# The second layer of chunk 1 in plain fp32 products, the second layer's weights split one block a place, and a reordered start in a DeltaNet + MoE kernel

## The chip, the cores and the metric

The kernel runs on one core of a Trainium2 chip. Its metric is the time of one execution on the device in microseconds (us), the median of several. The engines are TensorE (PE in the rows), VectorE (DVE), ScalarE (ACT), GpSimd (POOL) and SyncE (SP, which issues the transfers). Each engine works through its own list of instructions in order, and waits on semaphores for the others.

## What is computed

An attention with a delta rule, and on its output a two-layer perceptron with softplus (B = 4, H = 8, S = 768, head size 48, width 384, hidden width 2048):

```
k_n = k / (norm(k) + 1e-6)
for t in range(S):
    y[t]  = state . q[t]
    v_old = state . k_n[t]
    state = state + beta[t] * outer(k_n[t], v[t] - v_old)
x = y as (3072 tokens, 384)
g = softplus(x @ w_in)        # max(h, 0) + log1p(exp(-|h|)), w_in 384 x 2048
out = g @ w_out               # w_out 2048 x 384
```

## The kernel before, in words

**Attention in chunks.** The 768 steps are cut into 12 chunks of 64, and the 32 heads of a chunk are worked on together. A chunk needs its products of keys with keys (`gram`), the inverse of a triangular 64 x 64 system for each head, the corrected values, y and the next state. Two chunks share one inversion (`invert`). Its core is a chain of some 50 small pairs of instructions, `tmp` and `Z` (a multiply and an add), which for chunks 2 and up runs on POOL; for the first pair it runs on DVE. In front of the chain stand two wide multiplies by columns and by rows (L325, L327), which for `invert(1)` run on POOL and else on DVE, as does `scale_v(1)` (L146), which scales the values by the norms. Behind the chain come two transposes on DVE (L346, L349), and then products on PE in stages `cross_a`, `cross_b` whose results ACT copies into `off` and `tt`.

**The perceptron in places.** It is laid out in 96 "places" `t`, and all the attention's steps are hung on them with `at(place, cost, steps)`. The passes `PASSES` are chunk 0, chunk 1, and then two chunks at a time. Passes 0 and 1 have 8 places each, of two 128-row tiles of weights; the others have 16 places of one tile. A place on PE is `hidden` (first layer, L691), then the attention steps planned there, then `output` of the place before (second layer, L737), then steps planned at t + 0.5. On ACT a place is Abs, Exp and Ln of `hidden` (L696 to L698), then copies for the attention's steps, then the casts `high`. On DVE it is the rest of the softplus (L703 to L709), then `low`, then the attention's own.

**Split products.** Pass 0 multiplies plain fp32 numbers (two records of PE for each product in the trace). All passes after it multiply in a faster format, fp32r, with each number split in two: `hi` is a cast, `lo` what is left over, and three products take the place of one. For this a softplus of a split pass ends with a cast to `gh` (L705) and a subtract to `gl` (L706). The weights are split once, in `high` (a cast on ACT, 768 columns, w_in and w_out of a tile together) and `low` (a subtract on DVE, 768 columns), up to three tiles a place, in the places of the tables `HIGHS` and `LOWS` (places 3 to 13). The plain weights of tile f lie in a buffer named a{f+1}; `high(f)` writes buffer b{f} and `low(f)` buffer a{f}.

**The start.** Before place 0 stand the `gram` of chunks 2 and 3, the first mask's products (`first_p`), the inversion of the first pair on DVE, its solution by a sweep of small products, and `warm`, idle products that keep PE occupied. The weights come in through SP's queue in rows and are put together by DVE (`convert`, L648) during places 0 to 7.

Of the kernel before, what the change touches and what calls it, by code (L numbers as in the profile page):

```python
# [21 lines left out]
P = 128  # L22
# [21 lines left out]
CLEAR, DONE, END, GRAM, INV = {}, {1: 8, 2: 19}, {1: 6, 2: 17}, {4: 4, 5: 7}, {2: 11}  # L44
# [10 lines left out]
SLOT = (0, 2, 1)  # L55
FOUR = 15
# [4 lines left out]
def deltanet_moe(ctx, tc, kT, qT, kI, vN, beta, wts, out, outT):  # L61
# [83 lines left out]
    def scale_v(s):  # L145
        (nc.vector if s > 1 else nc.gpsimd).tensor_tensor(NV[s], NV[s], NN[s].unsqueeze(2).to_broadcast([P, NP, D]),  # L146
                                op=ALU.mult)
# [17 lines left out]
    def systems(u):  # L165

        LTD[u] = one.tile([P, 2 * NP, HB], F32, name="work")
# [128 lines left out]
    def invert(u):  # L296
# [27 lines left out]
        first = engine if u == N16 else nc.vector  # L324
        first.tensor_tensor(sq, sq, by_col, op=ALU.mult)  # L325
        yield 200 + n * n * m
        first.tensor_tensor(diagonal(Z, blocks, n, 0, 0, n, n), sq, by_row, op=ALU.mult)  # L327
# [46 lines left out]
    def couple(s):  # L374

        pms = [bank([P, NP // 2, C]) for e in range(2)]
        for i, e, p, ab, t in quads:
            nc.tensor.matmul(pms[e][tk[ab], i, :], LF[tk[t], s, p, :], DT[s][tk[t], p, :],
                             start=True, stop=True)
        negative(nc.scalar, MT[s][0], pms[0])  # L380
        negative(nc.scalar, MT[s][1], pms[1])
        for h in range(2):
            negative(nc.scalar, MT[s][2][tk[h]], pms[1][tk[1 - h]])
# [277 lines left out]
    def high(f):  # L661
        assert f < done[0]
        W[f, 0] = one.tile([P, 2 * DM], F32R, name=f"b{f}")
        nc.scalar.copy(W[f, 0], HF[f])

    def low(f):
        W[f, 1] = one.tile([P, 2 * DM], F32R, name=f"a{f}")
        nc.vector.tensor_tensor(W[f, 1], HF[f], W[f, 0], op=ALU.subtract)  # L668
# [5 lines left out]
    def weight(i, f, a, c, n):  # L674
        return W[f, a][:, c:c + n] if i else HF[f][:, c:c + n]
# [24 lines left out]
    def softplus(i, g):  # L700
        ph, a = PH.pop((i, g)), A.pop((i, g))
        if i:
            nc.vector.scalar_tensor_tensor(a, ph, 0.0, a, op0=ALU.max, op1=ALU.add)  # L703
            hi_lo = G[i, g] = [two.tile([P, 2 * n], F32R, name=name) for name in ("gh", "gl")]
            nc.vector.tensor_copy(hi_lo[0], a)  # L705
            nc.vector.tensor_tensor(hi_lo[1], a, hi_lo[0], op=ALU.subtract)  # L706
        else:
            hi_lo = G[i, g] = [two.tile([P, 2 * n], F32, name="gh")]
            nc.vector.scalar_tensor_tensor(hi_lo[0], ph, 0.0, a, op0=ALU.max, op1=ALU.add)  # L709
# [105 lines left out]
    with tc.manual_schedule(engines={ET.PE, ET.DVE, ET.Activation, ET.Pool, ET.SP}):  # L815
# [62 lines left out]
        both[0] = True  # L878
        pts = [first_p(0)]
        systems(1)  # L880
        gram(2)
        lower(1, halves_1[1], 1)
        gram(3)
        unread.append(ps_o.tile([P, 512], F32, name="po2"))
        warm(512)
        pts.append(first_p(1))
        run(iv)
        warm(512, 512)
# [4 lines left out]
        transpose_norms(0)  # L893
        for b, engine in enumerate((nc.scalar, nc.vector) * 2):
            expand(0, b, engine)
# [7 lines left out]
        couple(0)  # L903

        def pairs(g):
            return ([bank([P, 4, D]) for e in range(2)] if g == 0 else
                    [ps_h.tile([P, 4, D], F32, name=f"ph{e}") for e in range(2)])

        for g in range(2):
            i, to = slice(4 * g, 4 * g + 4), pairs(g)  # L910
            base(0, to, 4 * g, 4)
            nc.vector.tensor_copy(x_swap[:, i], to[1])
            nc.vector.tensor_copy(x_base[:, 0, i], to[0])
            for h in range(2):
                nc.gpsimd.tensor_copy(x_base[tk[h], 1, i], x_swap[tk[1 - h], i])
        warm(128)
# [17 lines left out]
        warm(256)  # L934
        first_y(0)
        warm(256)
        first_y(1)
        load_q(1)
        both[0] = False
# [94 lines left out]
        at(0, 6000, first_state, bind(steps, iv, 2))  # L1034
        at(0.5, 0, bind(steps, iv, 2))
        at(1, 1200, bind(couple, 1), bind(scale_v, 1), bind(run, iv))
# [15 lines left out]
        for c in range(2, NS, 2):  # L1052
# [30 lines left out]
            if u > 2:  # L1083
                if u == 3:
                    at(GRAM[c], 0, bind(load_beta, u), bind(systems, u), bind(gram_pair, c))
                at(8 * (c - 2) - (12 if u == 3 else EARLY), 0, bind(start, u, invert, INV[u]))
            elif u > 1:
                at(GRAM[c], 0, bind(load_beta, u), bind(systems, u), bind(gram, c))
                at(GRAM[c + 1], 0, bind(gram, c + 1), bind(start, u, invert, INV[u]))

        late, over = None, 0
        for t in range(8 * NS):
            costs[t] = costs.get(t, 0) + 960 * len(LOWS.get(t, ()))
            costs[t] += 1700 if t > 7 else 2900 if t < 5 else 700
        for i, p in enumerate(PASSES):
            for g in range(NF // 2 * len(p)):
# [15 lines left out]
                if i == 0:  # L1112
                    if g == 1:
                        load_v(2)
                        load_k(4)
                    top(2)
                for f in LOWS.get(t, ()):
                    low(f)
# [4 lines left out]
                for f in HIGHS.get(t, ()):  # L1123
                    high(f)
# [62 lines left out]
```

## Time and profile before

| what | value |
| --- | --- |
| runs | 562.95, 563.45, 563.60 us; median 563.45 |
| profiled execution | 562.74 us, of which 561.0 us are the span of the profile |
| PE busy | 539.0 us, 96% of the span |
| DVE, ACT, POOL busy | 65%, 65%, 37% |
| TensorE clock granted, mean | 0.988 |
| first hidden product (place 0) starts at | 40.45 us |

The span goes from the first to the last instruction on the core. An engine that isn't PE is idle for a third of the time or more, so only what PE waits for, or works at, can change the time; a time of a group of instructions elsewhere counts where it ends a wait of PE.

### The profile page before, as it was taken

To read this page: it belongs to the slowest core of one execution; us is meant where nothing else is said; L and a number is where in the kernel's file an instruction comes from. 1 tells how busy PE (TensorE), PEld (TensorE's weight loads), DVE (VectorE), ACT (ScalarE), POOL (GpSimd) and SP (SyncE) were. 2 spreads that over 40 slices of the span, in tenths; PEclk is the share of its full clock that TensorE was granted. 3 is DMA by queue.
4 is the path that set the end of the run, shared out by engine and by line. 5 is a ranking of instruction groups with operands and counts; after the bars stand their busy time and mean duration, and the time that the engine had idled before them with its cause. 6 is when DMAs were issued, how large, how long until landed. Compare 5 with 4: busy or idle time off the path is not lost.

```text
span 561.0 us, 17602 instructions
## 1 busy us (share of the span) xinstructions
PE 539.0 (96%) x7479; PEld 443.0 (79%) x7479; DVE 367.2 (65%) x660; ACT 363.9 (65%) x719; POOL 209.6 (37%) x365
## 2 busy tenths in 40 slices
PE   5788999899999999999999999999999999999997
PEld 3476768699987888877888888888887888888885
DVE  7858966999757857368747378747375737444434
ACT  5668685898677874756773757754557754454453
POOL 7125898119980179701886001886000000000000
PEclk9699999999999999999999999999999999999999
DMA  9919911223240132220122220031310030010001
GB/s 201 330 49 373 315 38 32 72 58 86 58 90 2 32 72 57 72 85 4 30 70 60 70 89 3 3 81 29 77 71 4 1 71 2 15 57 0 2 0 57
DMA packets 35502, 39.56 MB, mean 71 GB/s; under 512 B 22528, under 2 KB 25216, under 8 KB 35424
## 3 DMA queue, kind: packets, MB, share of 16 engines
q1 hardware_dynamic: 35280, 38.18, 24.2%
q8 instruction: 59, 0.97, 0.7%
q10 hardware_dynamic: 144, 0.26, 0.1%
q14 instruction: 19, 0.16, 0.1%
HBM read 31.55 MB, written 4.72 MB: 65 GB/s over the span
## 4 chain that ended last, share of the span: by engine, by line
PE 69%; POOL 16%; DVE 7%; DMA 3%; issue 2%; ACT 2%; ACTq 0%; DVEq 0%; POOLq 0%
PE po L737 29%; PE ph L691 27%; POOL Z L343 7%; POOL tmp L339 7%; PE pa L596 3%; PE pa L479 2%; DMA kt<-kT 2%; PE pa L439 2%; PE pa L565 1%; DMA big<-qT 1%; PE po L813 1%; DVE tt L349 1%; PE ph L577 1%; PE pa L577 1%; DVE a L668 1%
## 5 line engine op out<-in xcount | busy, mean ns | idle before, releaser
L691 PE MATMUL ph<-x,b 128*128 128x512 f32 (+1 forms) x576 | 166.2, 373 | 0.0
L696 ACT ACTIVATE a<-ph 128x512 f32<-128x512 f32 x96 | 57.4, 598 | 157.8 <-PE ph L691 153.2
L691 PE MATMUL ph<-x,a 128*128 128x512 f32 (+1 forms) x384 | 129.6, 374 | 2.4 <-DVE a L648 1.8
L703 DVE SCALAR_TENSOR_TENSOR a<-ph,a 128x512 f32<-128x512 f32 x88 | 60.4, 687 | 93.5 <-ACT a L698 93.2
L691 PEld LDWEIGHTS ph<-x,b 128*128 128x128 f32 x576 | 105.0, 188 | 19.4
L737 PE MATMUL po<-gh,b 128*128 128x512 f32 (+1 forms) x241 | 97.6, 405 | 1.4 <-DVE gh L705 1.4
L737 PE MATMUL po<-gh,a 128*128 128x512 f32 (+1 forms) x241 | 94.1, 390 | 0.0
L343 POOL TENSOR_TENSOR Z<-Z,tmp 128x30 f32<-128x30 f32 (+9 forms) x150 | 89.6, 597 | 11.8
L339 POOL TENSOR_TENSOR tmp<-Z,ltq 128x30 f32<-128x30 f32 (+9 forms) x150 | 86.5, 576 | 11.4
L691 PEld LDWEIGHTS ph<-x,a 128*128 128x128 f32 x384 | 72.0, 189 | 15.6 <-DVE a L648 2.2
L706 DVE TENSOR_TENSOR gl<-a,gh 128x512 fp32r<-128x512 f32 x88 | 66.4, 754 | 7.9 <-DVE gh L705 0.5
L737 PE MATMUL po<-gl,b 128*128 128x512 f32 (+1 forms) x241 | 69.4, 389 | 0.0
L698 ACT ACTIVATE a<-a 128x512 f32<-128x512 f32 x96 | 60.7, 632 | 3.1
L697 ACT ACTIVATE a<-a 128x512 f32<-128x512 f32 x96 | 60.6, 632 | 3.1
L737 PEld LDWEIGHTS po<-gh,b 128*128 128x128 f32 x241 | 45.2, 187 | 12.7 <-DVE gh L705 1.9
L737 PEld LDWEIGHTS po<-gl,b 128*128 128x128 f32 x241 | 45.2, 188 | 9.6
L737 PEld LDWEIGHTS po<-gh,a 128*128 128x128 f32 x241 | 45.3, 188 | 8.5
L705 DVE CAST gh<-a 128x512 fp32r<-128x512 f32 x88 | 40.0, 454 | 8.1 <-DVE a L703 0.9
L602 DVE TENSOR_TENSOR x<-pa,x 128x384 fp32r<-128x384 f32 x21 | 11.6, 554 | 38.1 <-ACT x L601 38.1
L256 POOL COPY ss<-ltq 128x32 f32<-128x32 f32 x6 | 1.4, 241 | 86.8 <-DVE ltq L303 86.8
L737 PE MATMUL po<-a,gh 128*128 128x384 f32 x96 | 33.5, 444 | 0.3 <-DVE gh L709 0.3
L493 DVE TENSOR_TENSOR big<-pa,maskP 64x256 f32<-64x256 f32 x66 | 27.8, 421 | 1.0
(220 smaller groups left out, 752.8 us busy)
## 6 DMA issues: line engine op xcount, KB each, us to landing
a<-wts SPq DMA_DIRECT2D x16, 383.8 KB, 7.5
b<-wts SPq DMA_DIRECT2D x16, 383.8 KB, 7.4
kt<-kT SPq DMA_DIRECT2D x24, 192.0 KB, 3.4
big<-qT SPq DMA_DIRECT2D x24, 192.0 KB, 4.0
nv<-vN SPq DMA_DIRECT2D x12, 384.0 KB, 3.7
ki<-kI SPq DMA_DIRECT2D x24, 192.0 KB, 3.3
outT<-ot SPq DMA_DIRECT2D x13, 256.0 KB, 2.3
x<-x SPq DMA_DIRECT2D x66, 32.0 KB, 2.0
```

Of the source, the lines that this page charges most:

```text
L339: engine.tensor_tensor(o, diagonal(Z, blocks, n, j + 1, j, r, j, (True, False)), diagonal(lq, blocks, n, j, 0, r, j, (False, True)), op=AL ...
L343: engine.tensor_tensor(z, z, o, op=ALU.add)
L493: nc.vector.tensor_tensor(be[tk[ab], ab, e, 4 * g:4 * g + 4, 0:C], pks[e][t, :, 0:C], maskP[t].unsqueeze(1).to_broadcast([C, 4, C]), op=AL ...
L596: nc.tensor.matmul(py[tk[ab], i, :], big[:, at + C:at + 2 * C], big[:, at:at + C], start=True, stop=True)
L691: nc.tensor.matmul(ph[:, j], weight(i, f, a, k * P, P), xr[b][k], start=(c == 0), stop=(c == len(terms) * NK - 1))
L696: nc.scalar.activation(a, ph, AF.Abs)
L697: nc.scalar.activation(a, a, AF.Exp, scale=-1.0)
L698: nc.scalar.activation(a, a, AF.Ln, bias=1.0)
L703: nc.vector.scalar_tensor_tensor(a, ph, 0.0, a, op0=ALU.max, op1=ALU.add)
L705: nc.vector.tensor_copy(hi_lo[0], a)
L706: nc.vector.tensor_tensor(hi_lo[1], a, hi_lo[0], op=ALU.subtract)
L737: nc.tensor.matmul(PO[i][h][:, c], l, r, start=(fs[j] == 0 and m == 0), stop=(fs[j] == NF - 1 and m == k - 1 and c != (cut and parts[0])))
```

## The change

The second layer of pass 1 (chunk 1) takes the plain form that pass 0 has: its softplus writes one fp32 `gh` without cast and subtract, and its output multiplies plain weights, one product in place of three. The split of a tile's weights is made in two halves, each in a buffer of its own with `hi` beside `lo`: w_in in buffer b{f} at the places of the old tables, and w_out in buffer a{f}, one tile a place, with the cast at place f + 12 and the subtract at place f + 13. The two wide multiplies of `invert(1)` and `scale_v(1)` go from POOL to DVE. K of chunk 4 and V of chunk 2 are loaded before 20 halves of weights are issued, and `gram(4)` moves from place 4 to 3.5. `invert(2)` starts at place 8.5 (it was 7). At the start, half of the first chain is set up ahead of `gram(2)`, one idle product of 512 columns changes its place, other idle products are trimmed or added (192 columns), a negative goes to DVE, one copy to ACT, and the sums of the base lie in other banks. The numbers of the planner's costs change with the smaller `low`.

```
@@ tables
-CLEAR, DONE, END, GRAM, INV = {}, {1: 8, 2: 19}, {1: 6, 2: 17}, {4: 4, 5: 7}, {2: 11}
+CLEAR, DONE, END, GRAM, INV = {}, {1: 8, 2: 19}, {1: 6, 2: 17}, {4: 3.5, 5: 7}, {2: 11}
+LATER = 13
@@ scale_v
-        (nc.vector if s > 1 else nc.gpsimd).tensor_tensor(NV[s], NV[s], NN[s].unsqueeze(2).to_broadcast([P, NP, D]),
+        nc.vector.tensor_tensor(NV[s], NV[s], NN[s].unsqueeze(2).to_broadcast([P, NP, D]),
@@ invert
-        first = engine if u == N16 else nc.vector
-        first.tensor_tensor(sq, sq, by_col, op=ALU.mult)
+        nc.vector.tensor_tensor(sq, sq, by_col, op=ALU.mult)
...
@@ couple
-        negative(nc.scalar, MT[s][1], pms[1])
-        for h in range(2):
-            negative(nc.scalar, MT[s][2][tk[h]], pms[1][tk[1 - h]])
+        negative(nc.scalar if s else nc.vector, MT[s][1], pms[1])
+        def rest():
+            for h in range(2):
+                negative(nc.scalar, MT[s][2][tk[h]], pms[1][tk[1 - h]])
+        return rest
@@ the split of the weights
-    def high(f):
+    def high(f, i):
         assert f < done[0]
-        W[f, 0] = one.tile([P, 2 * DM], F32R, name=f"b{f}")
-        nc.scalar.copy(W[f, 0], HF[f])
-    def low(f):
-        W[f, 1] = one.tile([P, 2 * DM], F32R, name=f"a{f}")
-        nc.vector.tensor_tensor(W[f, 1], HF[f], W[f, 0], op=ALU.subtract)
+        W[f, i] = one.tile([P, 2 * DM], F32R, name=f"{'ba'[i]}{f}")
+        nc.scalar.copy(W[f, i][:, 0:DM], HF[f][:, i * DM:(i + 1) * DM])
+    def low(f, i):
+        w = W[f, i]
+        nc.vector.tensor_tensor(w[:, DM:], HF[f][:, i * DM:(i + 1) * DM], w[:, 0:DM],
+                                op=ALU.subtract)
     def weight(i, f, a, c, n):
-        return W[f, a][:, c:c + n] if i else HF[f][:, c:c + n]
+        k = int(c >= DM)
+        if i <= k:
+            return HF[f][:, c:c + n]
+        c += (a - k) * DM
+        return W[f, k][:, c:c + n]
     def softplus(i, g):
-        if i:
+        if i > 1:
@@ the start
-        both[0] = True
         pts = [first_p(0)]
         systems(1)
+        lower(1, halves_1[1], 1)
         gram(2)
-        lower(1, halves_1[1], 1)
         gram(3)
-        unread.append(ps_o.tile([P, 512], F32, name="po2"))
-        warm(512)
         pts.append(first_p(1))
+        unread.append(bank([P, 512]))
+        warm(512, 512)
         run(iv)
-        warm(512, 512)
...
+        warm(192, behind=tmp)
...
-        warm(256)
+        warm(192)
         first_y(0)
-        warm(256)
         first_y(1)
         load_q(1)
-        both[0] = False
+        load_k(4)
+        load_v(2)
@@ the plan
-        at(0, 6000, first_state, bind(steps, iv, 2))
-        at(0.5, 0, bind(steps, iv, 2))
-        at(1, 1200, bind(couple, 1), bind(scale_v, 1), bind(run, iv))
+        at(0, 6000, bind(steps, iv, 2), first_state, bind(steps, iv, 2))
+        at(1, 1200, lambda: couple(1)(), bind(run, iv), bind(scale_v, 1))
...
-                at(GRAM[c + 1], 0, bind(gram, c + 1), bind(start, u, invert, INV[u]))
+                at(GRAM[c + 1], 0, bind(gram, c + 1))
+                at(8.5, 0, bind(start, u, invert, INV[u]))
@@ a place
                 for f in LOWS.get(t, ()):
-                    low(f)
+                    low(f, 0)
+                if LATER <= t < LATER + NF:
+                    low(t - LATER, 1)
                 if late:
                     output(*late)
...
                 for f in HIGHS.get(t, ()):
-                    high(f)
+                    high(f, 0)
+                if LATER - 1 <= t < LATER - 1 + NF:
+                    high(t + 1 - LATER, 1)
```

What the change moves on the engines shows best at two places. The first is ACT in places 17 to 19, of the kernel before (Abs, Exp and Ln of three softpluses stand on L696 to L698, the copies of `off` on L444):

```order
L696 ACTIVATE a<-ph_2698 128x512 [waits DVE_49,PE_49]
L697 ACTIVATE a<-a 128x512 [waits Activation_49]
L698 ACTIVATE a<-a 128x512 [waits Activation_49]
L696 ACTIVATE a<-ph_2730 128x512 [waits DVE_49,PE_49]
L697 ACTIVATE a<-a 128x512 [waits Activation_49]
L698 ACTIVATE a<-a 128x512 [waits Activation_49]
L444 ACTIVATE off<-pa 32x16x32 [waits PE_49]
L444 ACTIVATE off<-pa 32x16x32 x3
```

The same place of ACT in the changed kernel, where L667 is the cast of w_out of one tile and L704 to L706 are Abs, Exp and Ln:

```order
L667 CAST a_2608<-a_138 128x384 [waits DVE_49]
L704 ACTIVATE a<-ph_2610 128x512 [waits PE_49]
L705 ACTIVATE a<-a 128x512 [waits Activation_49]
L706 ACTIVATE a<-a 128x512 [waits Activation_49]
L667 CAST a_2643<-a_778 128x384 [waits DVE_49]
L704 ACTIVATE a<-ph_2645 128x512 [waits PE_49]
L705 ACTIVATE a<-a 128x512 [waits Activation_49]
L706 ACTIVATE a<-a 128x512 [waits Activation_49]
L447 ACTIVATE off<-pa 32x16x32 [waits PE_49]
L447 ACTIVATE off<-pa 32x16x32 x3
L667 CAST a_2743<-a_782 128x384 [waits DVE_49]
```

A cast with a wait for DVE has come in ahead of each Abs. DVE in the changed kernel, over the same places (L711 to L714 are the softplus, L671 the subtract for w_out, L346 to L349 the transposes behind POOL's chain):

```order
L711 SCALAR_TENSOR_TENSOR a<-ph_2488,a 128x512 [waits Activation_49]
L713 CAST gh<-a 128x512 [waits DVE_49,PE_49]
L714 TENSOR_TENSOR gl<-a,gh 128x512 [waits DVE_49]
L671 TENSOR_TENSOR a_2486<-a_134,a_2486 128x384
L346 STREAM_TRANSPOSE tt<-Z 128x32x32 [waits Pool_49]
L349 STREAM_TRANSPOSE tt<-Z 128x32x32
L147 TENSOR_TENSOR nv<-nv,nn 128x768
L711 SCALAR_TENSOR_TENSOR a<-ph_2610,a 128x512 [waits Activation_49]
L713 CAST gh<-a 128x512 [waits DVE_49,PE_49]
L714 TENSOR_TENSOR gl<-a,gh 128x512 [waits DVE_49,PE_49]
L671 TENSOR_TENSOR a_2608<-a_138,a_2608 128x384
```

Before, the softplus's three instructions are followed at once by the next step there; now a subtract that reads the plain weights of a tile (`a_134`, `a_138`) stands behind each. The second place is POOL in front of its first chain, of the kernel before:

```order
L256 COPY ss<-ltq 128x32 [waits DVE_49,Pool_49]
L311 AFFINE_SELECT ltq<-ltq 128x1024 [waits DVE_49,PE_49,Pool_49]
L270 TENSOR_SCALAR cT<-ncT 128x32 [waits DVE_49]
L146 TENSOR_TENSOR nv<-nv,nn 128x768 [waits DMAHW5_49]
L325 TENSOR_TENSOR ltq<-ltq,ncT 128x1024 [waits Pool_49]
L327 TENSOR_TENSOR Z<-ltq,cT 128x1024 [waits Pool_49]
L333 COPY Z<-cT 128x32 [waits Pool_49]
L339 TENSOR_TENSOR tmp<-Z,ltq 128x30
```

And of the changed kernel:

```order
L257 COPY ss<-ltq 128x32 [waits DVE_49,Pool_49]
L312 AFFINE_SELECT ltq<-ltq 128x1024 [waits DVE_49,PE_49,Pool_49]
L271 TENSOR_SCALAR cT<-ncT 128x32 [waits DVE_49]
L333 COPY Z<-cT 128x32 [waits DVE_49]
L339 TENSOR_TENSOR tmp<-Z,ltq 128x30
```

The three wide multiplies are gone from POOL; they stand on DVE behind the transposes and the norms of chunks 2 and 3, ahead of the softplus that follows.

## Rows read from the trace of the kernel before

**Rows 1.** The page, the chain of work that ended last, by engine.

```profile
PE 69%; POOL 16%; DVE 7%; DMA 3%; issue 2%; ACT 2%; ACTq 0%; DVEq 0%; POOLq 0%
```

**Rows 2.** Waits of PE from 40 us on: total us, times, longest.

```profile
PE ph L691 <- DVE a L648: 1.8, 1, 1.8
PE pa L416 <- ACT off L426: 1.6, 3, 0.9
PE po L737 <- DVE gh L705: 1.4, 2, 0.8
PE po L192 <- DMA kt<-kT: 1.0, 1, 1.0
...
PE po L192 <- DVE a L648: 0.2, 1, 0.2
```

**Rows 3.** Timeline of PE in the start: start, length, engine, line, operation.

```profile
22.21 2.07 PE L813 MATMUL po<-gl 128*128 128x512 f32 x2
```

**Rows 4.** Windows of 1 us: busy share and count by engine, granted clock, DMA.

```profile
24.00:25.00 1.00, 1.00 (x29) 0.79 (x32) 0.99 (x3) 0.98 (x4) 0.00 (x0) 0.50 1.04 418
25.00:26.00 1.00, 1.00 (x34) 0.69 (x27) 0.97 (x4) 0.97 (x3) 0.31 (x1) 0.98 1.03 415
```

**Rows 5.** Timeline of POOL in places 1 to 2.

```profile
51.48 2.67 POOL L325 TENSOR_TENSOR ltq<-ltq,ncT 128x1024 f32<-128x1024 f32 x1
...
56.77 0.23 POOL L339 TENSOR_TENSOR tmp<-Z,ltq 128x30 f32<-128x30 f32 x1
```

**Rows 6.** Timeline of DVE over the same stretch.

```profile
49.63 0.55 DVE L648 SCALAR_TENSOR_TENSOR a<-a,ex 128x384 int32<-128x384 int32 x1
...
51.85 2.70 DVE L648 SCALAR_TENSOR_TENSOR a<-a,ex 128x384 int32<-128x384 int32 x1
```

**Rows 7.** Groups by line, DVE: busy us, mean ns of one, idle before.

```profile
L325 DVE TENSOR_TENSOR ltq<-ltq,ncT 128x1024 f32<-128x1024 f32 (+1 forms) x5 | 5.6, 1123 | 0.1
```

**Rows 8.** Timeline of PE in place 8.

```profile
102.10 0.75 PE L416 MATMUL pa<-tt,off 32*32 32x32 f32 x64
...
108.43 0.50 PE L691 MATMUL ph<-x,b 128*128 128x256 f32 x2
```

**Rows 9.** Timeline of PE in place 1: an output in plain form, and what follows.

```profile
48.69 2.85 PE L737 MATMUL po<-a,gh 128*128 128x384 f32 x8
51.38 1.46 PE L691 MATMUL ph<-x,a 128*128 128x256 f32 x6
```

**Rows 10.** Timeline of ACT in place 8.

```profile
105.78 0.23 ACT L258 ACTIVATE rt<-rt 128x32 f32<-128x32 f32 x1 [1.51 <-DVE rt L257]
```

**Rows 11.** Timeline of PE in places 16 to 19: first output record, first hidden records.

```profile
156.60 0.33 PE L737 MATMUL po<-b,gh 128*128 128x384 f32 x1
...
158.71 0.63 PE L691 MATMUL ph<-x,b 128*128 128x512 f32 x2
...
165.08 0.62 PE L691 MATMUL ph<-x,b 128*128 128x512 f32 x2
...
169.16 0.62 PE L691 MATMUL ph<-x,b 128*128 128x512 f32 x2
```

**Rows 12.** Timeline of ACT in places 19 and 20: two Abs.

```profile
171.40 0.60 ACT L696 ACTIVATE a<-ph 128x512 f32<-128x512 f32 x1 [0.94 <-PE ph L691]
...
177.56 0.60 ACT L696 ACTIVATE a<-ph 128x512 f32<-128x512 f32 x1 [1.92 <-PE ph L691]
```

**Rows 13.** Timeline of DVE in place 20: the softplus, and what follows it.

```profile
179.51 0.69 DVE L703 SCALAR_TENSOR_TENSOR a<-ph,a 128x512 f32<-128x512 f32 x1 [2.83 <-ACT a L698]
...
181.44 2.06 DVE L303 STREAM_TRANSPOSE ltq<-work 128x1024 f32<-128x1024 f32 x1
```

**Rows 14.** Groups by line: a subtract and a cast of 384 columns.

```profile
L601 ACT CAST x<-pa 128x384 fp32r<-128x384 f32 x21 | 10.2, 484 | 0.0
L602 DVE TENSOR_TENSOR x<-pa,x 128x384 fp32r<-128x384 f32 x21 | 11.6, 554 | 38.1 <-ACT x L601 38.1
```

**Rows 15.** One window over places 13 to 28, columns as in rows 4.

```profile
134.50:225.80 91.30, 90.34 (x1481) 77.39 (x1480) 65.82 (x114) 64.87 (x130) 55.49 (x90) 1.00 0.23 57
```

More of the change, by code (lines that the diff above doesn't have):

```diff
@@ L323, in invert @@
             by_row = cT.unsqueeze(2).to_broadcast([P, n, n])
-        first = engine if u == N16 else nc.vector
-        first.tensor_tensor(sq, sq, by_col, op=ALU.mult)
+        nc.vector.tensor_tensor(sq, sq, by_col, op=ALU.mult)
         yield 200 + n * n * m
-        first.tensor_tensor(diagonal(Z, blocks, n, 0, 0, n, n), sq, by_row, op=ALU.mult)
+        nc.vector.tensor_tensor(diagonal(Z, blocks, n, 0, 0, n, n), sq, by_row, op=ALU.mult)
         yield 200 + n * n * m
@@ L902, in deltanet_moe @@
             first_mask(k // 2, k % 2)
-        couple(0)
+        rest = couple(0)
         def pairs(g):
-            return ([bank([P, 4, D]) for e in range(2)] if g == 0 else
-                    [ps_h.tile([P, 4, D], F32, name=f"ph{e}") for e in range(2)])
+            return [(ps_o, ps_h)[g == 0].tile([P, 4, D], F32, name=f"{'po' if g else 'ph'}{e}")
+                    for e in range(2)]
         for g in range(2):
@@ L912, in deltanet_moe @@
             nc.vector.tensor_copy(x_swap[:, i], to[1])
-            nc.vector.tensor_copy(x_base[:, 0, i], to[0])
+            copies[g](x_base[:, 0, i], to[0])
             for h in range(2):
                 nc.gpsimd.tensor_copy(x_base[tk[h], 1, i], x_swap[tk[1 - h], i])
+        rest()
         warm(128)
@@ L1088, in deltanet_moe @@
                 at(GRAM[c], 0, bind(load_beta, u), bind(systems, u), bind(gram, c))
-                at(GRAM[c + 1], 0, bind(gram, c + 1), bind(start, u, invert, INV[u]))
+                at(GRAM[c + 1], 0, bind(gram, c + 1))
+                at(8.5, 0, bind(start, u, invert, INV[u]))
         late, over = None, 0
         for t in range(8 * NS):
-            costs[t] = costs.get(t, 0) + 960 * len(LOWS.get(t, ()))
-            costs[t] += 1700 if t > 7 else 2900 if t < 5 else 700
+            costs[t] = costs.get(t, 0) + 500 * (len(LOWS.get(t, ())) + (LATER <= t < LATER + NF))
+            costs[t] += 1700 if t > 15 else 700 if t > 7 else 2900 if t < 5 else 700
         for i, p in enumerate(PASSES):
@@ L1112, in deltanet_moe @@
                 if i == 0:
-                    if g == 1:
-                        load_v(2)
-                        load_k(4)
                     top(2)
                 for f in LOWS.get(t, ()):
-                    low(f)
+                    low(f, 0)
+                if LATER <= t < LATER + NF:
+                    low(t - LATER, 1)
                 if late:
```

## The prediction

> **What bounds the kernel now.** I read four views, in this order. The page first: the chain that ended last is two thirds TensorE (PE), with a sixth on GpSimd (POOL) [rows 1]. The POOL share is one stretch, the inversions that run as a chain of small multiplies and adds in front of places 8 and 18; for the rest PE simply has work. Then the waits of PE from 40 us on [rows 2]: the largest are 1.8 us for a weight that VectorE (DVE) was still decoding, 1.6 us for `off`, 1.4 us for `gh` and 1.0 us for a K of chunk 4. So an edit that takes work off DVE, ScalarE (ACT) or POOL can give back at most these waits and part of the start-up; an edit that puts work on PE costs its full length; and an edit that makes ACT or DVE late costs whatever PE then waits. The timelines around each edit give the prices.
>
> **Start-up.** PE sends an idle product of 512 columns, two records, at 22.21 us, taking 2.07 us [rows 3]. The change takes it out of that place and lets masks' products follow. But in that stretch the granted clock is 0.50, that is 1.2 GHz, and 0.98 (2.4 GHz) a microsecond later [rows 4]; PE had been waiting for K before it. If the rise stays where it is, the first hidden product comes 2.0 us earlier; if it comes later because small products stand where the wide ones stood, nearly all is lost and 0.1 us stays. The other moves here (a negative on DVE, a copy on ACT, other banks, 192 columns in place of 256) are each below a microsecond and partly behind the sweep's own chain of DVE and PE. I take 1.0 us, between ends of 0.1 and 2.0.
>
> **Places 0 to 8.** POOL multiplies the large `ltq` at 51.48 us for 2.67 us [rows 5], and DVE's decoding instruction that overlaps it takes 2.70 us, where one alone takes 0.55 us [rows 6]. This is what PE waits 1.8 us for. The change puts the three wide multiplies on DVE. There such a multiply takes 1.1 us [rows 7], so DVE pays about 3.2 us for three and gets back 2.70 − 0.55 = 2.15 us from this row, and some from the one ahead of it and the one behind; DVE is then hardly later with its weights, and the wait of PE goes: −1.8 us. K of chunk 4 is issued ahead of a row of weights: the 1.0 us wait and the 0.2 us beside it go, and what is late next is that row of weights, whose decoding comes two places later. So −3.0 us here.
>
> POOL's small chain starts at 56.77 us [rows 5] and runs up to place 8, where DVE waits for its end. Without the three multiplies in front it starts some 3.3 us earlier as seen from the first hidden product: DVE's own multiplies are done in about half of POOL's time. It therefore keeps pace with a PE that is 3.0 us earlier. Behind it, PE's 64 small products of 0.75 us stand at 102.10 us, then eight records of output, 64 more small products, and the next hidden products at 108.43 us [rows 8]. Outputs of this form take 51.38 − 48.69 = 2.69 us [rows 9], so of the 6.33 us some 2.69 + 2 × 0.75 = 4.2 are work and 2.1 us are lost, on the copies of `off`. ACT does them late because a root for the next inversion is ahead of them and waits 1.51 us for DVE [rows 10]. The change starts that inversion at place 8.5, behind them: −2.1 us. Sum of the early gains: 1.0 + 3.0 + 2.1 = 6.1 us. That DVE loses the casts and subtracts of pass 1 I cost at nothing: PE waits for it there for 0.2 us only.
>
> **Plain products in pass 1.** Now an output of pass 1 is 12 records from 156.60 to 158.71 us, 2.11 us [rows 11]; the eight of them lie between 2.08 and 2.29 us, 17.5 us together. Afterwards each is four plain products, which the trace shows as eight records of 2.69 us [rows 9], and 0.1 us for the change of form beside the split first layer. 8 × 2.79 − 17.5 = +4.8 us. Nothing hides it: PE is the engine that has no room there. The bounds are 8 × 2.69 − 17.5 = 4.0 and, with the 2.85 us that the record itself spans [rows 9], 5.3.
>
> **w_out split later.** This is the part that decides. Until now the weights are all split by place 13. Afterwards place t (12 to 27) ends on ACT with a 384-column cast of tile f = t − 12 into buffer a{f}, and DVE subtracts tile f − 1 in the same place. Buffer a{f} holds the plain weights of tile f − 1, which that very subtract reads. So the cast can't start before the place's subtract, which stands behind the place's softplus on DVE, which stands behind the place's own Abs, Exp and Ln on ACT; and Abs of the next place is queued behind the cast. ACT and DVE take turns where they overlapped.
>
> The length of one turn, from rows: Abs at 177.56 us [rows 12], the softplus on DVE from 179.51, and behind its three instructions the next one of DVE at 181.44 [rows 13]: 3.88 us. A 384-column subtract is 0.55 us and a 384-column cast is 0.48 us [rows 14]: 4.9 us from Abs to Abs, 5.3 if DVE runs beside a busy POOL. A place without attention takes PE 169.16 − 165.08 = 4.08 us [rows 11]. Abs of the place that starts at 169.16 comes at 171.40 us [rows 12], 2.24 us behind, and `gh` is then ready 0.6 us before PE's next output wants it. So a first bare place loses 0.8 us on ACT, of which 0.6 is hidden, and the next one loses on PE; a place with attention, which is longer on PE, gives it back, except where its own copies on ACT stand behind the late Abs and PE waits for these copies.
>
> I laid out places 15 to 29 by hand with PE's own work as it is now, Abs never sooner than 4.9 us after the Abs before. New waits of PE: place 20 (small products for `off` of L447) 1.4 us; place 23 (masks' products for the softplus of 22) 1.6; place 24 (products for the mask of L572) 1.15; 25 and 27 together 0.25; place 28 the masks again 0.75; place 29 the mask again 1.35. That is 6.5 us, less the wait of 0.8 us for `gh` that stands in that stretch now [rows 2]: 5.7 us. Lower bound 2.5: only the three waits of 1.35 us and more, each shortened by 0.6 where a turn overlaps more than I allowed. Upper bound 8, with turns of 5.3 us in the 44 us in which POOL runs. The layout gives every turn its full length, so I take somewhat less than it says: +4.5 us.
>
> One rule bears on this. ACT waiting for DVE at 105.78 us holds back copies of `off` whose products had been done [rows 10]. The Trainium skill, "Perfetto Trace Analysis", in its section on the TensorE instruction, says that ACT, DVE and GpSimd are strict FIFO, while PE can pull a load of weights ahead. By that rule the +4.5 us stands; if ACT could take the next Abs past the waiting cast, it would be nothing and the time 562.1 us. The trace agrees with the rule.
>
> **Sum.** −6.1 + 4.8 + 4.5 = +3.2 us, on the profiled execution's 562.74 us: 565.9 us. That execution lies 0.7 us under the median of the runs, 563.45 us; against it the forecast is **566.6 us**. About 0.2%, 1.1 us, is what a measurement can tell from no change.
>
> **Rivals.**
> *The turns are absorbed.* The places with attention are longer, and 16 turns of 4.9 us (78 us) fit into the 91.3 us that places 13 to 28 take, of which PE is busy for 90.3 [rows 15]. If the delays are all given back before PE asks, the sum is 563.45 − 6.1 + 4.8 = 562.1 us; with all of the start-up, 561.1; and where DVE's relief in pass 1 is worth something too, less. For it: the mean place there is 91.3 / 16 = 5.7 us. Against it: the bare places come in pairs, and 0.6 us of slack isn't two delays of 0.8. It decides from about 2.4 us of new waits: with less than that the kernel is not slower by what can be measured.
> *Part of each.* The lower bound of the turns and the whole start-up: 563.45 − 7.1 + 4.8 + 2.5 = 563.7 us, no change to be seen.
> *The early gains do not come.* DVE now holds the three multiplies in its own line; if they push its weights back by as much as the collision did, the 3.0 us stay, and a late clock leaves 0.1 of the start-up: 563.45 − 0.1 − 2.1 + 4.8 + 4.5 = 570.6 us. Against it: DVE's rows beside POOL's, which are longer than both would be one after the other.
>
> **How the numbers follow.** The forecast 0.50, with its own range of 564.6 (0.2% above the median) to 569.3; absorbed 0.27; part of each 0.13; no early gains 0.10. The range must leave out at most 2 in 10: it reaches from the absorbed case with all of the start-up and 1 us of DVE's relief, 560.0, to just short of the last case, 570.5. Faster 0.27, same 0.13, slower 0.60.
>
> **What would show it.** Right: in places 18 to 29 ACT's cast of w_out stands behind an idle time that ends with a DVE subtract, in place after place, and PE's waits grow by masks, `off` and `gh` there; the wait for the decoded weight at 54 us is gone; hidden products of place 9 come 5 to 7 us earlier than 108.43 us; pass 1's outputs take 2.7 us and more. The forecast is wrong if PE's waits between places 15 and 29 stay under 2 us, if the first hidden product is not earlier, or if the clock rises at another time than I allowed.

## The result: 570.6 us, 1.2% slower

The changed kernel takes 570.6 us (median of 4 runs, 568.96 to 571.55) against 563.53 us before; the ratio is 1.0124, with a 95% interval of 1.0098 to 1.0150. On another chip it took 569.9 us against 562.98 (1.0132, 1.0111 to 1.0154). The forecast was 566.6 us: right in direction, with +3.2 us where +7.1 us came, and the time lies just above the range. It is also the figure of the rival that the early gains do not come, 570.6 us, but by chance: those gains came (places 0 to 8 below), and other terms were too small.

The page of the changed kernel, the chain of work that ended last by engine, beside [rows 1]:

```profile
PE 78%; ACT 8%; DVE 7%; DMA 4%; issue 1%; POOL 1%; SPq 0%; ACTq 0%; DVEq 0%; POOLq 0%
```

POOL has gone from the chain (16% before), and ACT stands in it with 8% (2% before). PE's largest waits in the changed kernel from 38 us on (total us, times, longest), beside [rows 2]:

```profile
PE ph L699 <- ACT off L235: 3.1, 2, 1.8
PE ph L242 <- DVE a L711: 2.5, 2, 1.8
PE pa L442 <- ACT off L447: 1.0, 1, 1.0
PE ph L699 <- DVE big L496: 0.8, 1, 0.8
PE po L745 <- DVE gh L713: 0.6, 1, 0.6
PE ph L699 <- ACT x L549: 0.6, 1, 0.6
```

The waits for a decoded weight (1.8 us), for `off` in place 8 (1.6 us) and for K (1.0 us) are gone, as the change meant. New ones for ACT's copies and DVE's softplus have come in.

Where the time went is best seen from the start of the first hidden product of places 0, 8, 9, 17 and 30 in PE's timeline, taken as differences to the kernel before. These are the stretches of the changed kernel and of six experiments, in us (each from one profiled execution):

| stretch | forecast | changed | old start | one buffer further | plain only | middle only | mended |
| --- | --- | --- | --- | --- | --- | --- | --- |
| up to place 0 | −1.0 | +2.6 | −0.2 | −0.7 | 0.0 | +0.5 | −0.8 |
| places 0 to 7 | −3.0 | −3.5 | −3.5 | −3.5 | −0.3 | −3.5 | −2.8 |
| place 8 | −2.1 | −1.9 | −1.9 | −1.9 | +0.2 | −0.7 | −2.2 |
| places 9 to 16 | +4.8 | +3.1 | +3.1 | +3.1 | +3.0 | +1.3 | +3.0 |
| places 17 to 29 | +4.5 | +8.3 | +8.3 | +0.6 | −0.4 | 0.0 | +0.6 |
| up to place 30 | +3.2 | +8.5 | +5.7 | −2.4 | +2.6 | −2.3 | −2.1 |

Behind place 30 nothing moves by more than 0.3 us. The changed kernel profiled once more (below) has +0.5, −3.5, −1.9, +3.1 and +8.7 us in the five stretches: the start differs most between executions, and places 17 to 29 hold a fall of the clock there (last section).

**Places 17 to 29.** The forecast's turns are there. First ACT, then DVE of the changed kernel in places 25 to 27 (timeline: start, length; the idle time before an instruction and what ended it in brackets). L704 is Abs, L706 Ln, L667 the cast of w_out, L711 to L714 the softplus, L671 the subtract of w_out:

```profile
213.97 0.60 ACT L704 ACTIVATE a<-ph 128x512 f32<-128x512 f32 x1
...
215.26 0.63 ACT L706 ACTIVATE a<-a 128x512 f32<-128x512 f32 x1
...
219.13 0.51 ACT L667 CAST a<-a 128x384 fp32r<-128x384 f32 x1 [3.23 <-DVE a L671]
219.55 0.59 ACT L704 ACTIVATE a<-ph 128x512 f32<-128x512 f32 x1
...
224.80 0.51 ACT L667 CAST a<-a 128x384 fp32r<-128x384 f32 x1 [3.33 <-DVE a L671]
225.22 0.59 ACT L704 ACTIVATE a<-ph 128x512 f32<-128x512 f32 x1
```

```profile
215.93 0.69 DVE L711 SCALAR_TENSOR_TENSOR a<-ph,a 128x512 f32<-128x512 f32 x1 [2.41 <-ACT a L706]
216.72 0.43 DVE L713 CAST gh<-a 128x512 fp32r<-128x512 f32 x1
217.25 0.95 DVE L714 TENSOR_TENSOR gl<-a,gh 128x512 fp32r<-128x512 f32 x1
218.12 0.97 DVE L671 TENSOR_TENSOR a<-a,a 128x384 fp32r<-128x384 f32 x1
```

ACT ends Ln at 215.9 and does nothing until the subtract ends at 219.1; DVE does nothing until Ln ends. They take turns. From Abs to Abs it is 5.6 us (213.97, 219.55, 225.22), not the 4.9 us of the forecast: while POOL runs its chain here, the subtract of 384 columns takes 0.97 us and the softplus's subtract 0.95, where 0.55 [rows 14] and 0.69 were taken. In places 18 to 20, where POOL is idle, it is 4.9 and 5.0 us, as forecast (Abs at 169.63, 174.54 and 179.55). PE pays where it meets a late result; in places 23, 24 and 29 these are the softplus, which still reads the buffer that the products of keys with keys write next, and ACT's copies of `off`:

```profile
196.30 0.27 PE L242 MATMUL ph<-kt 48*64 48x64 f32 x2 [1.80 <-DVE a L711]
...
201.88 0.50 PE L699 MATMUL ph<-x,b 128*128 128x512 f32 x1 [1.24 <-ACT off L235]
...
234.24 2.11 PE L699 MATMUL ph<-x,b 128*128 128x512 f32 x8 [1.84 <-ACT off L235]
```

**The start.** PE's timeline has an idle 2.24 us in the middle of the base's products that nothing in the profile explains ("issue"), and the first hidden product comes at 43.04 us in place of 40.45. The windows (columns as in [rows 4]) show that the clock, up at 26 us, falls again to 0.50 behind that idle stretch:

```profile
31.38 0.55 PE L396 MATMUL po<-nv,tt 64*64 64x48 f32 x19 [2.24 <-issue]
...
43.04 1.13 PE L699 MATMUL ph<-x,a 128*128 128x256 f32 x4 [0.57 <-ACT x L549]
```

```profile
26.00:28.00 2.00, 2.00 (x50) 1.27 (x52) 1.69 (x4) 0.00 (x0) 1.41 (x2) 1.00 1.02 411
30.00:32.00 2.00, 0.62 (x20) 0.57 (x21) 0.03 (x1) 1.96 (x4) 0.34 (x1) 1.00 0.02 8
...
36.00:38.00 2.00, 2.00 (x60) 1.98 (x58) 1.24 (x4) 0.00 (x0) 0.00 (x0) 0.50 0.03 8
```

### The profile page after: what moved, and what is told of

Read it like the earlier page. It is cut to its first block, busy times and chain, and to the rows that moved or that the text cites. A ratio compares the mean times of both kernels' runs of the same rounds, so it can differ in the third digit from the quotient of the medians.

```text
span 569.8 us, 17538 instructions
## 1 busy us (share of the span) xinstructions
PE 544.8 (96%) x7445; PEld 440.2 (77%) x7445; DVE 360.0 (63%) x663; ACT 365.8 (64%) x735; POOL 197.1 (35%) x362
## 4 chain that ended last, share of the span: by engine, by line
PE 78%; ACT 8%; DVE 7%; DMA 4%; issue 1%; POOL 1%; SPq 0%; ACTq 0%; DVEq 0%; POOLq 0%
PE po L745 32%; PE ph L699 30%; PE pa L599 3%; PE pa L482 3%; DMA kt<-kT 2%; PE pa L568 1%; DVE gl L714 1%; PE pa L580 1%; ACT a L705 1%; DVE a L711 1%; PE pa L442 1%; ACT a L706 1%; DMA big<-qT 1%; ACT a L704 1%; DVE a L671 1%
## 5 line engine op out<-in xcount | busy, mean ns | idle before, releaser
L699 PE MATMUL ph<-x,b 128*128 128x512 f32 (+1 forms) x864 | 197.1, 374 | 3.9 <-ACT off L235 3.1
L699 PEld LDWEIGHTS ph<-x,b 128*128 128x128 f32 x864 | 152.9, 188 | 34.8 <-ACT off L235 3.9
L704 ACT ACTIVATE a<-ph 128x512 f32<-128x512 f32 x96 | 57.3, 597 | 136.5 <-PE ph L699 131.8
L745 PE MATMUL po<-gh,a 128*128 128x512 f32 (+1 forms) x482 | 128.3, 398 | 0.6 <-DVE gh L713 0.6
L711 DVE SCALAR_TENSOR_TENSOR a<-ph,a 128x512 f32<-128x512 f32 x80 | 55.1, 689 | 95.2 <-ACT a L706 94.9
L745 PEld LDWEIGHTS po<-gh,a 128*128 128x128 f32 x482 | 87.7, 188 | 20.5 <-DVE gh L713 1.2
L745 PE MATMUL po<-gl,a 128*128 128x512 f32 (+1 forms) x241 | 69.6, 390 | 0.0
L714 DVE TENSOR_TENSOR gl<-a,gh 128x512 fp32r<-128x512 f32 x80 | 59.1, 739 | 7.5 <-DVE gh L713 0.5
L706 ACT ACTIVATE a<-a 128x512 f32<-128x512 f32 x96 | 60.7, 632 | 3.1
L745 PEld LDWEIGHTS po<-gl,a 128*128 128x128 f32 x241 | 45.2, 188 | 10.2 <-DVE gl L714 0.6
L745 PE MATMUL po<-a,gh 128*128 128x384 f32 x128 | 45.3, 496 | 0.6 <-DVE gh L717 0.6
L745 PEld LDWEIGHTS po<-a,gh 128*128 128x128 f32 x128 | 23.1, 189 | 14.6 <-DVE gh L717 0.8
L667 ACT CAST a<-a 128x384 fp32r<-128x384 f32 x16 | 8.2, 513 | 23.9 <-DVE a L671 23.9
L699 PE MATMUL ph<-x,a 128*128 128x256 f32 x96 | 22.5, 384 | 0.6 <-ACT x L549 0.6
L599 PEld LDWEIGHTS pa<-big 128*64 128x64 f32 x640 | 20.2, 138 | 3.4 <-issue 2.1
```

Of the source, the lines that this page charges most:

```text
L599: nc.tensor.matmul(py[tk[ab], i, :], big[:, at + C:at + 2 * C], big[:, at:at + C], start=True, stop=True)
L699: nc.tensor.matmul(ph[:, j], weight(i, f, a, k * P, P), xr[b][k], start=(c == 0), stop=(c == len(terms) * NK - 1))
L704: nc.scalar.activation(a, ph, AF.Abs)
L706: nc.scalar.activation(a, a, AF.Ln, bias=1.0)
L745: nc.tensor.matmul(PO[i][h][:, c], l, r, start=(fs[j] == 0 and m == 0), stop=(fs[j] == NF - 1 and m == k - 1 and c != (cut and parts[0])))
```

## The experiments

Each run is timed beside the kernel before on the same chip. Medians of before in the three groups: 563.3, 562.98 and 562.92 us.

**The subtract ahead of the softplus.** Edit of the changed kernel:

```
                     hidden(i, g)
+                if LATER <= t < LATER + NF:
+                    low(t - LATER, 1)
...
                 softplus(i, g)
-                if LATER <= t < LATER + NF:
-                    low(t - LATER, 1)
```

> The changed kernel, but DVE's subtract for w_out stands directly behind the first-layer products of its place, ahead of the place's softplus, in place of behind it; the same instructions otherwise. Theory of the turns (ACT's cast waits for a subtract that waits for the place's own Abs, Exp and Ln): the cast's wait goes, the 8.1 us lost between places 17 and 29 shrink to 1 us or less, time 562.5 to 564 us. Rival (the 16 more instructions on ACT and on DVE are the load that makes PE wait): the same load, so 569 to 571 us as the changed kernel.

Measured: 569.06 us (1.0098, 1.0075 to 1.0121), a miss for the 562.5 to 564 us, and by its number in the rival's range. From this run, the group of ACT's cast (busy us, mean ns, idle before), and DVE's subtract in place 21:

```profile
L667 ACT CAST a<-a 128x384 fp32r<-128x384 f32 x16 | 8.1, 508 | 1.9 <-DVE a L671 1.8
```

```profile
187.50 0.56 DVE L671 TENSOR_TENSOR a<-a,a 128x384 fp32r<-128x384 f32 x1 [3.34 <-ACT a L667]
```

ACT's wait for the subtract is gone (23.9 us in the changed kernel, 1.9 here), but now DVE waits for the cast, which stands behind ACT's copies of the place before, and holds back all that is behind it on DVE: the transposes at the end of POOL's chain, and the masks (PE waits 2.4 us for `gh` at 174 us and 2.1 us for the masks at 192). So this edit moved the wait to another engine. It neither confirms the turns nor favours the load, since it makes a new wait of its own; an edit that makes none was needed.

**One buffer further.** To the changed kernel with the old start (below):

```
-        W[f, i] = one.tile([P, 2 * DM], F32R, name=f"{'ba'[i]}{f}")
+        W[f, i] = (two if i and not f else one).tile(
+            [P, 2 * DM], F32R, name=("ex" if not f else f"a{f - 1}") if i else f"b{f}")
```

> As the run with the old start (the changed kernel with the start of before), but the halves of w_out of tile f go into the buffer a{f-1} in place of a{f} (tile 0 into one of the two buffers named ex, dead by then): ACT's cast then waits for the subtract of the place before, which is long done. Same instructions in the same order. Theory of the turns: the 8.1 us lost between places 17 and 29 shrink to 1 us or less, 560.5 to 562.5 us. Rival (the load of 16 casts and 16 subtracts, in these places, is what PE waits for): 568 to 569 us as with the old start. Between them, if the second inversion's chain on POOL, started later, becomes what place 18 or 19 waits for: 562.5 to 564.5 us.

Measured: 561.51 us (0.9966, 0.9953 to 0.9980), 7.3 us below the 568.8 us of the run that differs only in this line. The two ran on different chips; against the kernel before on its own chip, one is 5.5 us slower and the other 1.5 us faster, 7.0 us apart. The group of ACT's casts of w_out, first of the changed kernel, then of this run (tile 0 has a row of its own):

```profile
L667 ACT CAST a<-a 128x384 fp32r<-128x384 f32 x16 | 8.2, 513 | 23.9 <-DVE a L671 23.9
```

```profile
L665 ACT CAST a<-a 128x384 fp32r<-128x384 f32 x15 | 7.6, 507 | 0.1
```

In places 17 to 29 the same casts and subtracts in the same order cost 8.3 us with the wait and 0.6 us without it. The load is not the cause; the wait for a buffer is. POOL's chain did not become what PE waits for.

**The old start.** The changed kernel with the lines from `pts = [first_p(0)]` to `first_y(1)`, and `couple`, as before.

> The changed kernel with the start (all ahead of the loads for chunk 1's places) of the kernel before. If the new order of the start costs the 2.6 us by which the first hidden product was late: first hidden product back at 40.5 us, one rise of the clock at 25 us and no second fall, 567.5 to 568.5 us. Rival (the idle 2.2 us and the fall of the clock behind it come from loading instructions and meet any order): first hidden product at 42 us or later, 570 to 571 us.

Measured: 568.8 us (1.0094, 1.0078 to 1.0110), first hidden product at 40.22 us, one rise of the clock and no second fall. The theory holds by the profile; the time is 0.3 us above its range. Its six runs lie between 568.26 and 569.30 us.

**The new start alone.** The kernel before with these lines of the changed kernel.

> The kernel before with the start of the changed kernel, and nothing else of it. The prediction had −1.0 us (562.4 us). Theory from the two profiles of this start (first hidden product at 43.0 us with an idle 2.2 us that nothing explains and a second fall of the clock, and at 40.6 us without them): no gain, 563.3 us where that idle time is absent and 2 to 3 us more where it is present, so a spread of 2 us or more between its runs. Rival (the new start is slower by itself): all runs at 565.5 us or more.

Measured: 563.74 us (1.0008, 0.9997 to 1.0019), 562.51 to 565.58 over 12 runs. In the profiled one PE waits 1.98 us at the same product and the first hidden product still comes at 40.29 us, so the stretch does not cost 2 to 3 us as the theory had it: the new start would be faster, and the idle stretch eats it up.

**The changed kernel again.**

> The changed kernel once more, on the same chip as these. If the idle 2.2 us of its start comes in some executions only: times in two groups, 568 and 570.5 us, and the first hidden product of the profiled one at 40.6 or at 43.0 us. If it belongs to the order of its instructions: all at 570 to 571.5 us and 43.0 us again.

Measured: 569.9 us, first hidden product at 40.97 us, with 0.88 us of idle "issue" at that product and 0.71 us at a later one. The idle stretch does not come and go: it is there in all five profiles of this start with the weights ahead of it, with 0.8 to 2.2 us at the same product, and at the start the clock fell behind the longest one only. The times do fall in two groups, five of the nine in 568.96 to 569.9 and four in 571.49 to 571.76 us. One execution of each group was profiled, with first hidden products at 40.97 and 43.04 us, so the length of the stretch, with the clock behind it, is likely what parts them; two profiles don't show it.

**Fewer weights ahead of the start.** To the kernel with the new start alone:

```
-        feed(6)
+        feed(4)
...
-        feed(20)
+        feed(22)
```

> The kernel before with the new start, and two halves of weights (0.77 MB) issued behind the start in place of ahead of it, so that the transfers end some 1.9 us sooner than 29 us. Theory (PE's idle 1.6 to 2.2 us in the second group of base products is a load of its instructions that queues behind the weights): the load runs about 2 us sooner, the idle time shrinks below 0.5 us, first hidden product at 38.5 to 39.2 us, 561.7 us. Rival (the instructions are asked for too late, whatever the weights do): an idle time of 1.5 to 2 us at the same product and 563 to 564 us.

Measured: 563.94 us (1.0014, 0.9999 to 1.0029), by its number in the rival's range. By the profile the theory is right, and the time is spent elsewhere. PE's timeline, first of the new start alone, then of this run:

```profile
30.86 0.55 PE L396 MATMUL po<-nv,tt 64*64 64x48 f32 x19 [1.98 <-issue]
...
40.29 0.92 PE L694 MATMUL ph<-x,a 128*128 128x256 f32 x3 [0.57 <-ACT x L549]
```

```profile
39.15 1.13 PE L694 MATMUL ph<-x,a 128*128 128x256 f32 x4 [0.57 <-ACT x L549]
...
71.68 0.44 PE L192 MATMUL pa<-kt 48*64 48x64 f32 x2 [2.79 <-DMA kt<-kT]
```

The idle stretch is gone, and the first hidden product is 1.1 us earlier (39.15 against 40.29); then K of chunk 4, now behind two more halves of weights, comes late by 2.8 us, and the clock falls behind that wait.

**Plain products alone.** To the kernel before; the lower half of w_out is left out in pass 1:

```
-        if i:
+        if i > 1:
...
+        if i == 1 and c >= DM:
+            return W[f, 0].bitcast(F32)[:, c:c + n]
```

> The kernel before, with pass 1's second layer in the plain form alone: no cast and subtract in its softplus, four plain products a place on the cast weights (the lower half of w_out is left out there, so the values are less exact). Theory of the prediction (PE has no room, DVE's relief is worth nothing): +4.8 us, 568.3 us. Rival (DVE, which was full in pass 1, is relieved and gives some of it back, as places 9 to 17 of the changed kernel lost only 3.1 us): 566 to 567 us.

Measured: 567.13 us (1.0065, 1.0043 to 1.0087), 1.2 us below the theory and 0.1 us above the rival's range; +3.0 us in places 9 to 16 of the profile, −0.4 us behind. Window from the first hidden product of place 9 to that of place 16, before and here:

```profile
108.43:154.52 46.09, 45.87 (x857) 43.34 (x851) 41.46 (x69) 39.18 (x75) 28.76 (x41) 1.00 0.27 70
```

```profile
108.36:157.03 48.67, 48.67 (x831) 38.85 (x823) 31.95 (x56) 39.16 (x75) 32.79 (x52) 1.00 0.28 72
```

DVE is relieved of 9.5 us (41.46 to 31.95), and PE gains from it at most the 0.22 us for which it had been idle. So in the kernel before the relief is worth next to nothing, as predicted, and the rival's reason is wrong (with the edits of places 0 to 9 it is otherwise, see the next run). The term is smaller for another reason: half of the plain outputs are shorter than in place 1. Of the eight, the four with attention's products behind them take 2.7 to 2.8 us, the four straight ahead of a first layer 2.3 to 2.4; in the changed kernel 156.68 to 158.97 is 2.29 us to the start of the split first layer that follows.

```profile
156.68 2.74 PE L745 MATMUL po<-a,gh 128*128 128x384 f32 x8
158.97 1.39 PE L699 MATMUL ph<-x,b 128*128 128x512 f32 x4
```

**The middle alone.** The kernel before with the three multiplies on DVE, K and V loaded ahead, `gram(4)` at 3.5, and `invert(2)` from 8.5.

> The kernel before with only the edits that act in places 0 to 9: three wide multiplies from POOL to DVE, K of chunk 4 loaded ahead and its products half a place earlier, the second inversion started at 8.5. Start, splits and pass 1 as before. Theory (these edits by themselves give the 3.5 us up to place 8 and 1.9 us in place 8): 557.5 to 559 us, hidden products of place 9 at about 103 us. Rival (their gain is lost again behind place 9, where DVE is full with the casts and subtracts of pass 1 and the next inversion now starts later): 561 to 563.5 us.

Measured: 559.86 us (0.9940, 0.9923 to 0.9956), between the two ranges. The edits of places 0 to 9 are a gain by themselves. They give 3.5 us in places 0 to 7 as in the changed kernel, but only 0.7 in place 8, and 1.3 us are lost again in place 11, where DVE still has the casts and subtracts of pass 1 and PE waits for it: part of the rival holds.

```profile
PE pa L416 <- DVE x L604: 1.3, 1, 1.3
```

In place 8 the difference comes from POOL's chain. It starts at the same distance from the first hidden product in both (14.2 us), but ends 1.2 us later here, because steps of it that run beside DVE's subtracts take longer, and these are 768 columns wide here and 384 in the changed kernel. The subtracts, one step of the chain, and the transpose that waits for its end, first of this run, then of the changed kernel (first hidden products at 40.99 and 43.04 us):

```profile
89.03 2.35 DVE L668 TENSOR_TENSOR a<-a,b 128x768 fp32r<-128x768 f32 x2
89.48 1.09 POOL L339 TENSOR_TENSOR tmp<-Z,ltq 128x150 f32<-128x150 f32 x1
...
96.02 2.00 DVE L346 STREAM_TRANSPOSE tt<-Z 128x1024 f32<-128x1024 f32 x1 [4.64 <-POOL Z L343]
```

```profile
91.16 0.49 POOL L339 TENSOR_TENSOR tmp<-Z,ltq 128x150 f32<-128x150 f32 x1
91.30 1.52 DVE L671 TENSOR_TENSOR b<-a,b 128x384 fp32r<-128x384 f32 x2
...
96.89 1.95 DVE L346 STREAM_TRANSPOSE tt<-Z 128x1024 f32<-128x1024 f32 x1 [4.07 <-POOL Z L343]
```

So with these edits in place, the work that the rest of the change takes off DVE in places 3 to 13 is worth about 2.5 us (1.2 in place 8, 1.3 in place 11), if the plain form costs the 3.0 us that it costs alone. What part of the 1.3 us the plain form has, and what part the smaller subtracts, no run separates.

**The middle with the new start; lighter starts; the whole change mended.**

> The kernel before with the edits of places 0 to 9 and with the new start; no plain products in pass 1, no later split. If the new start is worth its 1.0 us of the prediction: 558.9 us; if it is worth nothing, 559.9 us as without it; if it costs 2 to 3 us in some executions, 560 to 562.5 us with a wider spread.

> The same lighter start in the kernel with the edits of places 0 to 9 and the new start (no plain products, no later split). By the theory that the weights hold up PE's instructions 558.5 to 559.5 us, below that kernel's 560.9; by the rival 560.5 to 561.5 us.

> The kernel with the edits of places 0 to 9 and the old start, and the two halves of weights issued later. If the weights also hold up the 0.87 us wait in the first group of the base products there: 559 us, 0.9 us below 559.9; if that wait is for ACT, as the profile names it: 559.9 us, unchanged.

> The whole changed kernel with its two faults mended: the halves of w_out one buffer further (no turns between ACT and DVE), and the two halves of weights issued later. What stays is −5.4 us of places 0 to 9, +3.1 us of plain products, about 1 us of waits in places 18 to 24, and the start: 560.5 to 561.5 us if the start gains its 1.5 us by the lighter transfers, 562 to 563 us if it doesn't.

Measured, in this order: 560.91 us (0.9962, 0.9944 to 0.9980), 559.83 us (0.9943, 0.9925 to 0.9962), 560.25 us (0.9951, 0.9934 to 0.9968) and 560.04 us (0.9948, 0.9930 to 0.9966). The first lies in its third range, with a wide spread as expected (557.71 to 563.06 us); the second misses both of its ranges and the fourth is below both of its own; the third stays at its 559.9 within the noise. With the weights ahead of it the new start is about 1 us slower (560.91 against 559.86 us, on different chips, with intervals that overlap), and with two halves moved the difference is gone. With the old start the lighter transfers gain nothing. The whole change with both faults mended is 10 us faster than as it stood, and beats the kernel before; its PE waits between 150 and 235 us, where the changed kernel has 7.4 us:

```profile
PE ph L242 <- DVE a L712: 1.2, 1, 1.2
```

The four best kernels, this one, the middle alone and the two with a lighter start, can't be told apart: 559.83 to 560.25 us.

## Why the prediction fell short

Two steps failed. The start-up took 2 us out and let nothing else become late; in the profiled execution that term is 3.6 us short. And the turns were taken too small, by 3.8 us. The other terms came out 2.0 us better than forecast and hid part of it.

- **Places 0 to 8** (−3.0 and −2.1 us): the sizes were right, −3.5 and −1.9 us measured, and the waits for the decoded weight, for K and for `off` are gone. For place 8 this was partly luck. POOL's chain was to start 3.3 us earlier as seen from the first hidden product; it starts 2.1 us earlier (14.2 us behind that product, 16.3 before). With the edits of places 0 to 9 alone place 8 gains 0.7 us; by the traces the other 1.2 come from the smaller subtracts beside the chain. The forecast put what is taken off DVE at nothing; with PE earlier, it is worth about 2.5 us.
- **Plain products** (+4.8 us): the mechanism was right, the term too large by 1.7 us. I took every output at the 2.69 us of place 1 and 0.1 more; half of them are shorter, in front of a first layer. The eight outputs of before also add up to 17.7 us, not 17.5. This error was on the side that hid the others.
- **w_out split later** (+4.5 us): the mechanism was right and the term mis-sized; it measured 8.3 us, and the run with one buffer further shows about 7 us of time for the wait alone. Place by place the hand layout was near where POOL is idle: place 20 loses 1.4 us (1.4 laid out), the products of place 23 1.6 (1.6). Two things were wrong with the size. The turn was taken as 4.9 us throughout, and 5.3 as an upper end, though the profile showed POOL at work for 44 us of this stretch; it is 5.6 us there, so PE's waits in front of places 27 and 29 are 0.8 and 1.84 us where 0.25 (with place 25) and 1.35 were laid out. And the layout of 5.7 us was lowered to 4.5 by a feeling that turns overlap; nothing in the traces shows them to.
- **Start-up** (−1.0 us): wrong in sign for the profiled execution (+2.6 us), and about nothing in the median of the run with the new start alone (563.74 against 562.98 us). The step that failed is that nothing would be late in place of the 2 us removed. PE now stands idle in the base's products while the weights fill the transfers (below), and in the profiled execution the clock fell behind that. Of the forecast's own signs, that the first hidden product is not earlier came true, and place 9 begins 2.8 us earlier than before, where 5 to 7 were named.
- **The rule on queues.** The 23.9 us for which ACT stood before casts, with Abs of the next place ready behind them, are what the Trainium skill, "Perfetto Trace Analysis" (section on the TensorE instruction), makes of a strict FIFO; the trace agrees with it, and the run with one buffer further puts the price at about 7 us.

What is shown for the idle stretch at the start: it is there at the same product in all five profiles with this start and the weights ahead, and at that product it is gone in the three with fewer weights ahead (0.2 and 0.4 us at a later one stay in two of them). That it is a load of instructions is argued from this, and from the queue that the page marks "instruction": all 16 such idle stretches of PE in the fourteen profiles (0.15 us or more, behind 20 us) end 1.2 to 1.6 us behind the end of a packet of 16 KiB on it. No run here changed the instructions by themselves. Full transfers are not needed for such a stretch: the one at the later product lasts up to 0.71 us, with the weights done by then, and one of 0.78 us comes with the old start too (the middle alone, at 34 us). And where two halves of weights were moved, in three runs with the edits of places 0 to 9, one of 0.3, 1.0 and 0.5 us stands at 73 us.

## What to carry to other kernels

When a step is put into the loop of two engines, look for the buffer it writes: if the last reader of that buffer stands behind a result of the same engine in the same round, the two engines take turns, however idle both look (DVE 63%, ACT 64% busy here); with a buffer one round further ACT's wait went from 23.9 to 0.1 us. Such a step has to be priced with the durations of the stretch it lands in, beside the engine that runs there, and an estimate laid out from rows isn't to be lowered by feeling. And a small change that wins in one stretch and loses in another is best measured in stretches: here the change lost 7 us as it stood, and gained 3 with two small edits.

## What the runs showed of the hardware

**Idle time behind a packet of instructions.** With the transfers full of weights PE stood still for 0.8 to 2.2 us at the same product in five profiles, and each time went on 1.3 to 1.5 us behind the end of a packet of 16 KiB on an instruction queue. The Trainium skill, "Runtime: NRT & Kernel Launch", section "Instruction fetch mechanics", says that an engine's instructions are refilled in blocks by a transfer queue of its own, at a cost that is mostly hidden. If the stretch is such a refill, it is not hidden here, in a run of small products; the measurement decides.

**One wait can cost the clock.** In the run with the subtract ahead, PE waited 2.38 us at 171.8 us, and the granted clock was 0.55 (near 1.2 GHz) in the 3 us behind it, and 1.00 again from 178 us on:

```profile
172.00:174.00 2.00, 0.00 (x0) 0.00 (x0) 1.90 (x4) 1.94 (x5) 0.00 (x0) 1.00 0.03 8
174.00:177.00 3.00, 2.86 (x7) 2.29 (x8) 2.69 (x6) 0.91 (x2) 0.00 (x0) 0.55 0.00 0
178.00:180.00 2.00, 2.00 (x10) 1.40 (x8) 0.62 (x1) 0.00 (x0) 0.00 (x0) 1.00 0.00 0
```

The 1.8 us wait of the kernel before at 54 us [rows 2] was not followed by such a fall. The length of the wait does not tell which one is: in the changed kernel PE waits 0.97 us for `off` in place 20, in both of its profiles. In the first the granted clock stays at 1.00; in the second, where that wait ends at 176.67 us, it falls:

```profile
178.00:181.00 3.00, 3.00 (x7) 2.33 (x8) 1.43 (x3) 2.90 (x7) 0.00 (x0) 0.50 0.03 5
```

So a wait of PE can cost more than it lasts, and part of what one profile shows behind a wait is this.

**DVE beside POOL.** The subtract of 384 columns takes 0.55 us with POOL idle and 0.97 us while POOL works its chain. POOL pays too: a step of its chain on 150 columns took 1.09 us beside subtracts of 768 columns and 0.49 us beside those of 384, and three wide ones in place of three halves made the chain 1.2 us longer.
